# Storing the high and low halves of every stationary matmul operand by turns, element by element

## The chip, the core and the metric

The program runs on one core of one Trainium2 chip. The metric is the device time of one execution in microseconds; the time of the kernel is the median of several executions. A core has TensorE (PE, with its weight loads shown apart as PEld), VectorE (DVE), ScalarE (ACT), GpSimd (POOL) and SyncE (SP), which here only starts transfers. All of them work on SBUF, the on-chip memory of 128 partitions; TensorE writes to PSUM, a smaller memory of 128 partitions.

A matmul on TensorE has two operands in SBUF. The **stationary** one (`lhsT` in the code) is first loaded into the array by a weight load of its own, here 128 columns. The **moving** one (`rhs`) is then streamed past it, one column after the other; its number of columns is the second number of a shape such as 128x256 in the profile.

## The reference

Sliding-window attention with a few sink positions, and behind it a two-layer network with the gate h - tanh(h):

```python
B, H, S, D = 4, 8, 768, 64            # n_sink 4, window 128
scores = q @ k.T / sqrt(D)
keep = is_sink | ((rel >= 0) & (rel < window))
a = softmax(where(keep, scores, -1e9))
x = (a @ v) as [B * S, H * D]         # 3072 tokens x 512
h = x @ w_in                          # 512 -> 2048
g = h - tanh(h)
out = g @ w_out                       # 2048 -> 512
```

## The kernel before

**Splitting numbers.** The inputs are fp32. TensorE has a four-byte type, F32R (`float32r`), that goes through the array in one pass and keeps fewer bits. To keep the accuracy, an operand X is cut into a high part Xh (X cast to F32R) and a low part Xl = X - Xh, and a product is taken as three: Xh Yh + Xl Yh + Xh Yl. ScalarE does the cast (the functions called `high`), VectorE the subtraction (`low`).

**Tiling.** The 3072 tokens are 12 chunks of 256. A chunk's attention is four units, one for each pair of heads. The 2048 inner columns of the network are 8 groups of 256. A *step* is one (chunk, group); there are 96, in the order of lines 262 to 264: the first group for chunks 0, 1 and 2, then chunks 2 and 1 by turns through groups 1 to 7, then chunk 0, then chunks 3 to 11 one after the other.

A step has, on TensorE, 24 matmuls of the first product (`mm1`, line 695: stationary is a 128x128 piece of the first weights, high, high and low; moving is 256 columns of x, high, low and high), written to the PSUM tile h. Then the gate (lines 697 to 717): ACT takes tanh of h (L700), DVE subtracts (L703), ACT casts the result to the high part gh (L707), DVE makes the low part gl (L711). Then come 12 matmuls of the second product (`mm2`, line 743: stationary is a 128x128 piece of gh or gl, moving is 512 columns of the second weights). The first eight of them need only gh, the last four need gl. TensorE does the first product of step n + 1 before the second product of step n.

In the attention, the scores of the units from 12 on are made with F32R as well (line 491: stationary is 128 columns of the split queries qh or ql, moving is 260 columns of the split keys ks). The first twelve units use fp32 as it is (line 484). Lines 570, 601, 618 and 624 are transposes and the product with v.

**Where the halves lie.** The weights come from memory as 64-bit words and are decoded by three DVE instructions (lines 163, 165, 167), which read every second 32-bit word of `wraw`. Then `high` (L671) and `low` (L676) write one tile of [128, 2, 1024]: all the high parts, then all the low parts. gh and gl are two tiles of [128, 2, 256] each. The split queries are one tile of [128, 2, 2, 256], the high half first. In all of these a stationary piece of 128 columns is 128 neighbouring words.

**Order.** A planner (`Work`, lines 176 to 237) gets every piece of work with its engine, a duration and a due time, and lays out a fixed order for each engine. The waits between the engines come from the tiles that the instructions read and write, as the framework sees them.

Of the kernel before, what the change touches and what calls it, by code (L numbers as in the profile page):

```python
# [9 lines left out]
F32 = mybir.dt.float32  # L10
F32R = mybir.dt.float32r
# [3 lines left out]
ALU = mybir.AluOpType  # L15
# [3 lines left out]
P = 128  # L19
DM = H * D  # L20
DFF = 2048
NPAIR = H // 2
# [3 lines left out]
WIN = TS + P  # L26
KW = WIN + TS
KPACK = P + NT * TS
CH = 2 * P
# [5 lines left out]
WG = 2 * DM  # L35
# [134 lines left out]
def _decode(nc, m, t):  # L170
    lo, hi = (w.bitcast(U32) for w in _words(t))
    for i in range(3):
        _decode_part(nc, m.bitcast(U32), lo, hi, i)


class Work:
# [63 lines left out]
def _banded(tc, qd, kp, vp, vs, masks, w_in, w_out, ident, pts, early, out):  # L240
    nc = tc.nc
    et = mybir.EngineType
    with ExitStack() as ctx:
# [195 lines left out]
        def split(u):  # L439

            def k_high(h):
                if h == 0:
                    t = hpool.tile([P, NPAIR * CH], F32R, tag="ha", name=f"ks{u}")
                    ks[u] = t[:, : 2 * KW].rearrange("p (h k) -> p h k", h=2)
                r = slice(64 * h, 64 * h + 64)
                nc.scalar.copy(ks[u][r, h, :], kt[u][r, :])

            def k_low(h):  # L450
                k, t = ks[u], kt[u]
                r, o = slice(64 * h, 64 * h + 64), slice(64 * (1 - h), 64 * (1 - h) + 64)
                nc.vector.tensor_tensor(k[o, h, :], t[r, :], k[r, h, :].bitcast(F32), op=ALU.subtract)  # L453

            def q_high():
                t = hpool.tile([P, 2, 2, CH], F32R, tag="hb", name=f"q{u}")
                qh[u], ql[u] = t[:, 0], t[:, 1]
                nc.scalar.copy(qh[u], qt[u])  # L458

            def q_low():  # L460
                nc.vector.tensor_tensor(ql[u], qt[u], qh[u].bitcast(F32), op=ALU.subtract)

            t = due_unit(u) - 5000
            k, q = ([s] for s in slots(u))
            old = [("x", 2)] + [("xu", 2, i) for i in range(NPAIR)] if u == 3 * NPAIR else []
            work.add("ACT", 525, t, q_high, q, ["qh"] + old)
            work.add("DVE", 705, t, q_low, q + ["qh"], ["ql"], port=True)
            for h in range(2):
                work.add("ACT", 425, t, lambda h=h: k_high(h), k, [("ks", h)] + old)
                work.add("DVE", 590, t, lambda h=h: k_low(h), k, [("ks", h)], port=True)  # L470

        def scores(u, t):
            cc, p, b, c = unit(u)
            kind = min(2 * c + t, 2)
            apart = u < TWO and t == 1

            def products():
                where, tag = (ps_o, "o") if apart else (ps_s, "s")
                both = where.tile([P, 2, 512], F32, tag=tag, name=f"s{u}_{t}")
                ps = [both[:, h, :] for h in range(2)]  # L480
                sps[u, t] = both, ps
                for h in range(2):
                    if raw(u):
                        nc.tensor.matmul(
                            ps[h][:, :WIN], lhsT=qt[u][:, h, t * P : (t + 1) * P],
                            rhs=kt[u][:, t * TS : t * TS + WIN], start=True, stop=True,
                        )
                        continue
                    rhs = ks[u][:, h, t * TS : t * TS + WIN]
                    for i, q in enumerate((qh[u], ql[u])):  # L490
                        nc.tensor.matmul(  # L491
                            ps[h][:, :WIN], lhsT=q[:, h, t * P : (t + 1) * P], rhs=rhs,
                            start=i == 0, stop=i == 1,
                        )

            def merge():
                both, ps = sps[u, t]
                if t == 0:
                    where, tag = (wmpool, "wm") if slot(u) > 1 else (pp, "p")
                    pr[u] = where.tile([P, 4, TS], F32, tag=tag, name=f"p{u}")  # L500
                    st[u] = sm.tile([P, 12], F32, tag="st", name=f"st{u}")
                if kind > 0:
                    nc.vector.copy_predicated(  # L503
                        both[:, :, TS:WIN], above.bitcast(U32).unsqueeze(1).to_broadcast([P, 2, P]),
                        both[:, :, :P],
                    )
                for h in range(2):
                    j = 2 * h + t
                    nc.vector.tensor_tensor_reduce(  # L509
                        out=pr[u][:, j, :], in0=ps[h][:, P:WIN], in1=mask[:, kind, :], scale=-0.125,  # L510
                        scalar=BIG, op0=ALU.add, op1=ALU.min, accum_out=st[u][:, j : j + 1],
                    )

            def exponent():
                for j in (t, 2 + t):
                    e = pr[u][:, j, :]
                    nc.scalar.activation(  # L517
                        e, e, AF.Exp, bias=st[u][:, j : j + 1], scale=-1.0,
                        accum_out=st[u][:, 4 + j : 5 + j],
                    )  # L520

            d = due_unit(u) + 500 * t
            s = ["o0", "o1"] if apart else ["s0", "s1"]
            if raw(u):
                src, took = slots(u), 890
            else:
                src, took = ["qh", "ql", ("ks", 0), ("ks", 1)], 490
            work.add("PE", took, d, products, src, s)
            work.add("DVE", 880 if kind else 450, d + 1000, merge, s + ["mask"] * (0 < kind), [("p", slot(u), i) for i in range(t, 2)])
            work.add("ACT", 780, d + 2000, exponent, (), [("p", slot(u), t)])  # L530
# [128 lines left out]
        def weights(k, g):  # L659
            key, r = (k, g), count[0] % 2  # L660
            count[0] += 1

            wm[key] = pts[:, 2 + r].rearrange("p h a b -> p (h a b)")

            def bits(i):
                lo, hi = (w.bitcast(U32) for w in _words(wraw[key]))
                _decode_part(nc, wm[key].bitcast(U32), lo, hi, i)

            def high():
                t = wpool.tile([P, 2, WG], F32R, tag=f"w{k}_{g}", name=f"w{k}_{g}")  # L670
                nc.scalar.copy(t[:, 0, :], wm[key])  # L671
                wt[key] = t.rearrange("p a (d f) -> p a d f", d=(NPAIR, 2)[k])

            def low():
                t = wt[key].rearrange("p a d f -> p a (d f)")
                nc.vector.tensor_tensor(t[:, 1, :], wm[key], t[:, 0, :].bitcast(F32), op=ALU.subtract)  # L676

            d = due_group(g) + WNEXT * k - WLEAD
            for i in range(3):
                work.add("DVE", (684, 1224, 1224)[i], d, lambda i=i: bits(i), [("wr", k, g, 0), ("wr", k, g, 1)], [("dw", r)], port=True)  # L680
            work.add("ACT", 985, d + 1000, high, [("dw", r)], [("w", *key)])
            work.add("DVE", 1224, d + 1500, low, [("dw", r)], [("w", *key)], port=True)
# [4 lines left out]
        def mm1(n, k):  # L687
            cc, g = order[n]
            if k == 0:
                hps[n] = ps_h.tile([P, 2, CH], F32, tag="h", name=f"h{n}")  # L690
            f, r = divmod(k, 12)
            d, t = divmod(r, 3)
            w = wt[0, g][:, (0, 0, 1)[t], d, f * P : (f + 1) * P]
            x = (xh, xl, xh)[t][cc][:, d, :]
            nc.tensor.matmul(hps[n][:, f, :], lhsT=w, rhs=x, start=r == 0, stop=r == 11)  # L695

        def gate(n):
# [5 lines left out]
                nc.vector.tensor_tensor(hps[n], hps[n], gr[n], op=ALU.subtract)  # L703

            def high():
                gh[n] = gpool.tile([P, 2, CH], F32R, tag="gh", name=f"gh{n}")
                nc.scalar.copy(gh[n], hps[n])  # L707

            def low():
                gl[n] = gpool.tile([P, 2, CH], F32R, tag="gl", name=f"gl{n}")  # L710
                nc.vector.tensor_tensor(gl[n], hps[n], gh[n].bitcast(F32), op=ALU.subtract)  # L711

            d, h, r = due_step(n), ("h", n % 2), n % 2
            work.add("ACT", 510, d, tanh, [h], ["gr"])
# [19 lines left out]
        def mm2(n, k):  # L734
            cc, g = order[n]
            first, last = g == 0, g == NG - 1

            low, r = divmod(k, 8)
            t, r = divmod(r, 2 if low else 4)
            f, i = (r, 2) if low else divmod(r, 2)  # L740
            if first and not low and r == 0:
                ops[cc, t] = sums_of(n, cc, t)
            nc.tensor.matmul(  # L743
                ops[cc, t], lhsT=(gh, gh, gl)[i][n][:, f, t * P : (t + 1) * P],
                rhs=wt[1, g][:, (0, 1, 0)[i], f, :],
                start=first and not low and r == 0, stop=bool(last and low and r == 1),
            )

# [300 lines left out]
```

## Time and profile before

| | us |
|---|---|
| median of 3 executions | 691.68 |
| lowest, highest | 691.46, 692.03 |
| profiled execution, its span | 689.9 |
| PE busy in it | 677.0 |
| PEld busy | 599.9 |
| DVE busy | 427.5 |
| ACT busy | 367.0 |

The profile shows one execution; 1.8 us of the median lie around its span. A matmul's own duration in the profile (0.28 us for 256 columns) is longer than the distance from one matmul to the next, because they are pipelined; what a matmul costs is read from the length of a row of many of them in the chain of work that ended last. PEld is busy beside PE: while one matmul streams, the weights of the next are loaded.

### The profile page before, as it was taken

The page shows a single profiled execution, that of the slowest core. Times are in us where ns is not written, and L with a number is a line of the kernel's source. Part 1 is how long each engine was busy: PE and PEld are TensorE (multiplying, and loading weights), DVE is VectorE, ACT ScalarE, POOL GpSimd, SP SyncE. Part 2 cuts the span into 40 slices and gives each one's busy share as a digit, 9 for nine tenths or more (in the row PEclk, how much of TensorE's full clock was granted, in tenths as well). Part 3 has the DMA queues.
Part 4 walks back from the last instruction along what each step waited for, and adds up shares of the span by engine and source line. Part 5 has one row for each costly group of instructions (what it writes and reads, how often), then busy time and mean ns, then how long its engine had stood idle before and what let it go on. Part 6 is the DMA issues. An engine that isn't in the chain of part 4 may idle for free.

```text
span 689.9 us, 12423 instructions
## 1 busy us (share of the span) xinstructions
PE 677.0 (98%) x4604; PEld 599.9 (87%) x4604; DVE 427.5 (62%) x1084; ACT 367.0 (53%) x1001; POOL 52.0 (8%) x201
## 2 busy tenths in 40 slices
PE   7999999999999999999999999999999999999996
PEld 5777899999889889889988988998898898988985
DVE  7889999847755747556646665565564755663221
ACT  5996433347655646456555655555465545644222
POOL 6220010000000010000001000001000000000000
PEclk9999999999999999999999999999999999999999
DMA  6789800022130121112113112112112212100001
GB/s 205 241 273 384 314 1 5 1 88 55 55 89 28 43 92 55 28 49 84 39 28 109 55 27 90 29 53 85 32 42 75 55 28 61 55 1 1 31 1 35
DMA packets 31713, 52.14 MB, mean 76 GB/s; under 512 B 3228, under 2 KB 21020, under 8 KB 31644
## 3 DMA queue, kind: packets, MB, share of 16 engines
q1 hardware_dynamic: 31340, 50.93, 23.3%
q8 instruction: 38, 0.62, 0.4%
q10 hardware_dynamic: 304, 0.33, 0.2%
q14 instruction: 31, 0.25, 0.1%
HBM read 44.96 MB, written 6.29 MB: 74 GB/s over the span
## 4 chain that ended last, share of the span: by engine, by line
PE 90%; DVE 3%; ACT 3%; SPq 1%; issue 1%; POOL 1%; DMA 0%; POOLq 0%; DVEq 0%; ACTq 0%
PE o L743 39%; PE h L695 38%; PE s L491 5%; PE x L624 5%; PE t L570 2%; ACT p L543 1%; ACT p L517 1%; PE x L618 1%; DVE pt L584 1%; DVE pt L167 1%; DMA qk<-kp 0%; DVE p L509 0%; DVE pt L165 0%; PE x L601 0%; SPq L104 0%
## 5 line engine op out<-in xcount | busy, mean ns | idle before, releaser
L695 PE MATMUL h<-xh,w 128*128 128x256 f32 x1536 | 286.9, 280 | 0.0
L695 PEld LDWEIGHTS h<-xh,w 128*128 128x128 f32 x1536 | 241.1, 188 | 1.9 <-issue 0.2
L695 PE MATMUL h<-xl,w 128*128 128x256 f32 x768 | 214.6, 279 | 0.0
L743 PE MATMUL o<-w,gh 128*128 128x512 f32 x768 | 199.5, 400 | 0.7 <-ACT gh L707 0.6
L743 PEld LDWEIGHTS o<-w,gh 128*128 128x128 f32 x768 | 137.5, 188 | 28.9 <-ACT gh L707 1.5
L695 PEld LDWEIGHTS h<-xl,w 128*128 128x128 f32 x768 | 144.2, 188 | 1.7
L743 PE MATMUL o<-w,gl 128*128 128x512 f32 x384 | 106.8, 398 | 0.0
L700 ACT ACTIVATE graw<-h 128x512 f32<-128x512 f32 x96 | 57.0, 594 | 91.1 <-PE h L695 91.0
L517 ACT ACTIVATE p<-p,st 128x132 f32<-128x132 f32 x192 | 76.1, 398 | 52.6 <-DVE st L509 51.7
L711 DVE TENSOR_TENSOR gl<-h,gh 128x512 fp32r<-128x512 f32 x96 | 66.1, 688 | 48.7 <-ACT gh L707 48.5
L703 DVE TENSOR_TENSOR h<-h,graw 128x512 f32<-128x512 f32 x96 | 66.4, 692 | 44.9 <-ACT graw L700 44.2
L743 PEld LDWEIGHTS o<-w,gl 128*128 128x128 f32 x384 | 70.8, 188 | 16.9 <-issue 1.0
L707 ACT CAST gh<-h 128x512 fp32r<-128x512 f32 x96 | 55.6, 579 | 49.6 <-DVE h L703 49.5
L503 DVE COPY_PREDICATED s<-above,s 128x256 f32<-128x256 uint32 x80 | 34.0, 425 | 75.3 <-PE s L491 74.7
L543 ACT ACTIVATE p<-p,st 128x132 f32<-128x132 f32 x192 | 62.0, 396 | 5.7 <-DVE st L538 5.3
L509 DVE CUSTOM_DVE_ANT_0 p<-s,mask 128x132 f32<-128x132 f32 x192 | 49.0, 292 | 8.2 <-POOL qraw L342 2.1
L548 POOL CAST z<-p 128x16 fp32r<-128x16 f32 x48 | 10.2, 213 | 499.9 <-ACT p L543 498.0
L458 ACT CAST q<-qraw 128x512 fp32r<-128x512 f32 x36 | 22.4, 622 | 45.9 <-PE s L491 43.9
L491 PE MATMUL s<-ks,q 128*128 128x260 f32 x288 | 46.3, 283 | 0.0
L491 PEld LDWEIGHTS s<-ks,q 128*128 128x128 f32 x288 | 42.5, 188 | 4.2
L640 DVE TENSOR_TENSOR xl<-x,xh 128x512 fp32r<-128x512 f32 x24 | 16.5, 689 | 44.9 <-ACT xh L636 44.9
L453 DVE TENSOR_TENSOR ks<-kraw,ks 64x392 fp32r<-64x392 f32 x72 | 40.4, 561 | 2.2
(80 smaller groups left out, 573.8 us busy)
## 6 DMA issues: line engine op xcount, KB each, us to landing
qraw<-qd SPq DMA_DIRECT2D x36, 256.0 KB, 2.7
wraw<-w_in SPq DMA_DIRECT2D x16, 512.0 KB, 8.2
wraw<-w_out SPq DMA_DIRECT2D x16, 512.0 KB, 10.5
kraw<-kp SPq DMA_DIRECT2D x37, 196.0 KB, 2.6
v<-vp SPq DMA_DIRECT2D x27, 256.0 KB, 2.9
out<-ob SPq DMA_DIRECT2D x24, 256.0 KB, 2.2
qk<-kp SPq DMA_DIRECT2D x8, 196.0 KB, 5.1
qk<-qd SPq DMA_DIRECT2D x16, 64.0 KB, 4.9
```

The lines of the kernel that those rows point to most:

```text
L453: nc.vector.tensor_tensor(k[o, h, :], t[r, :], k[r, h, :].bitcast(F32), op=ALU.subtract)
L491: nc.tensor.matmul(ps[h][:, :WIN], lhsT=q[:, h, t * P : (t + 1) * P], rhs=rhs, start=i == 0, stop=i == 1,)
L509: nc.vector.tensor_tensor_reduce(out=pr[u][:, j, :], in0=ps[h][:, P:WIN], in1=mask[:, kind, :], scale=-0.125, scalar=BIG, op0=ALU.add, op1 ...
L517: nc.scalar.activation(e, e, AF.Exp, bias=st[u][:, j : j + 1], scale=-1.0, accum_out=st[u][:, 4 + j : 5 + j],)
L543: nc.scalar.activation(pr[u][:, j, :], pr[u][:, j, :], AF.Copy, scale=s[:, 8 + j : 9 + j])
L624: nc.tensor.matmul(xps[key][(p - p0) // 2][h * 64 : h * 64 + 64, p % 2, a:z], lhsT=vt[cc, i][:, hd : hd + D], rhs=rhs, start=False, stop=p ...
L695: nc.tensor.matmul(hps[n][:, f, :], lhsT=w, rhs=x, start=r == 0, stop=r == 11)
L700: nc.scalar.activation(gr[n], hps[n], AF.Tanh)
L703: nc.vector.tensor_tensor(hps[n], hps[n], gr[n], op=ALU.subtract)
L707: nc.scalar.copy(gh[n], hps[n])
L711: nc.vector.tensor_tensor(gl[n], hps[n], gh[n].bitcast(F32), op=ALU.subtract)
L743: nc.tensor.matmul(ops[cc, t], lhsT=(gh, gh, gl)[i][n][:, f, t * P : (t + 1) * P], rhs=wt[1, g][:, (0, 1, 0)[i], f, :], start=first and no ...
```

## The change

Each stationary operand that comes in two halves is stored so that element i of the high half lies at word 2i and element i of the low half at word 2i + 1 of one tile. This concerns the first weights (`k` = 0), the gate's values (gh and gl become one tile `g`) and the split queries. A stationary piece of 128 columns is now 128 words with a step of two. ACT and DVE write the halves with the same step, and DVE reads the high half with it. The second weights, which are the moving operand, stay as they were, as do x and the keys. The numbers and the order of instructions given to the planner are unchanged.

```diff
--- before.py
+++ after.py
@@ -173,6 +173,12 @@
         _decode_part(nc, m.bitcast(U32), lo, hi, i)
 
 
+def _by_turns(t):
+
+    w = t.rearrange("p (n z) -> p n z", z=2)
+    return w[:, :, 0], w[:, :, 1]
+
+
 class Work:
 
 
@@ -453,12 +459,13 @@
                 nc.vector.tensor_tensor(k[o, h, :], t[r, :], k[r, h, :].bitcast(F32), op=ALU.subtract)
 
             def q_high():
-                t = hpool.tile([P, 2, 2, CH], F32R, tag="hb", name=f"q{u}")
-                qh[u], ql[u] = t[:, 0], t[:, 1]
-                nc.scalar.copy(qh[u], qt[u])
+                t = hpool.tile([P, 4 * CH], F32R, tag="hb", name=f"q{u}")
+                qh[u], ql[u] = _by_turns(t)
+                nc.scalar.copy(qh[u], qt[u].rearrange("p h s -> p (h s)"))
 
             def q_low():
-                nc.vector.tensor_tensor(ql[u], qt[u], qh[u].bitcast(F32), op=ALU.subtract)
+                q = qt[u].rearrange("p h s -> p (h s)")
+                nc.vector.tensor_tensor(ql[u], q, qh[u].bitcast(F32), op=ALU.subtract)
 
             t = due_unit(u) - 5000
             k, q = ([s] for s in slots(u))
@@ -489,7 +496,7 @@
                     rhs = ks[u][:, h, t * TS : t * TS + WIN]
                     for i, q in enumerate((qh[u], ql[u])):
                         nc.tensor.matmul(
-                            ps[h][:, :WIN], lhsT=q[:, h, t * P : (t + 1) * P], rhs=rhs,
+                            ps[h][:, :WIN], lhsT=q[:, (2 * h + t) * P : (2 * h + t + 1) * P], rhs=rhs,
                             start=i == 0, stop=i == 1,
                         )
 
@@ -667,13 +674,13 @@
                 _decode_part(nc, wm[key].bitcast(U32), lo, hi, i)
 
             def high():
-                t = wpool.tile([P, 2, WG], F32R, tag=f"w{k}_{g}", name=f"w{k}_{g}")
-                nc.scalar.copy(t[:, 0, :], wm[key])
-                wt[key] = t.rearrange("p a (d f) -> p a d f", d=(NPAIR, 2)[k])
+                t = wpool.tile([P, 2 * WG], F32R, tag=f"w{k}_{g}", name=f"w{k}_{g}")
+                wt[key] = (t[:, :WG], t[:, WG:]) if k else _by_turns(t)
+                nc.scalar.copy(wt[key][0], wm[key])
 
             def low():
-                t = wt[key].rearrange("p a d f -> p a (d f)")
-                nc.vector.tensor_tensor(t[:, 1, :], wm[key], t[:, 0, :].bitcast(F32), op=ALU.subtract)
+                high, low = wt[key]
+                nc.vector.tensor_tensor(low, wm[key], high.bitcast(F32), op=ALU.subtract)
 
             d = due_group(g) + WNEXT * k - WLEAD
             for i in range(3):
@@ -690,7 +697,7 @@
                 hps[n] = ps_h.tile([P, 2, CH], F32, tag="h", name=f"h{n}")
             f, r = divmod(k, 12)
             d, t = divmod(r, 3)
-            w = wt[0, g][:, (0, 0, 1)[t], d, f * P : (f + 1) * P]
+            w = wt[0, g][(0, 0, 1)[t]][:, (2 * d + f) * P : (2 * d + f + 1) * P]
             x = (xh, xl, xh)[t][cc][:, d, :]
             nc.tensor.matmul(hps[n][:, f, :], lhsT=w, rhs=x, start=r == 0, stop=r == 11)
 
@@ -703,12 +710,13 @@
                 nc.vector.tensor_tensor(hps[n], hps[n], gr[n], op=ALU.subtract)
 
             def high():
-                gh[n] = gpool.tile([P, 2, CH], F32R, tag="gh", name=f"gh{n}")
-                nc.scalar.copy(gh[n], hps[n])
+                t = gpool.tile([P, 4 * CH], F32R, tag="g", name=f"g{n}")
+                gh[n], gl[n] = _by_turns(t)
+                nc.scalar.copy(gh[n], hps[n].rearrange("p f s -> p (f s)"))
 
             def low():
-                gl[n] = gpool.tile([P, 2, CH], F32R, tag="gl", name=f"gl{n}")
-                nc.vector.tensor_tensor(gl[n], hps[n], gh[n].bitcast(F32), op=ALU.subtract)
+                h = hps[n].rearrange("p f s -> p (f s)")
+                nc.vector.tensor_tensor(gl[n], h, gh[n].bitcast(F32), op=ALU.subtract)
 
             d, h, r = due_step(n), ("h", n % 2), n % 2
             work.add("ACT", 510, d, tanh, [h], ["gr"])
@@ -741,8 +749,8 @@
             if first and not low and r == 0:
                 ops[cc, t] = sums_of(n, cc, t)
             nc.tensor.matmul(
-                ops[cc, t], lhsT=(gh, gh, gl)[i][n][:, f, t * P : (t + 1) * P],
-                rhs=wt[1, g][:, (0, 1, 0)[i], f, :],
+                ops[cc, t], lhsT=(gh, gh, gl)[i][n][:, (2 * f + t) * P : (2 * f + t + 1) * P],
+                rhs=wt[1, g][(0, 1, 0)[i]][:, f * DM : (f + 1) * DM],
                 start=first and not low and r == 0, stop=bool(last and low and r == 1),
             )
```

## The prediction

> **What bounds the kernel now.** I read the page's busy table first, then its shares of the chain that ended last, then the table of stretches.
>
> ```profile
> span 689.9 us, 12423 instructions
> PE 677.0 (98%) x4604; PEld 599.9 (87%) x4604; DVE 427.5 (62%) x1084; ACT 367.0 (53%) x1001; POOL 52.0 (8%) x201
> PE o L743 39%; PE h L695 38%; PE s L491 5%; PE x L624 5%; PE t L570 2%; ACT p L543 1%; ACT p L517 1%; PE x L618 1%; DVE pt L584 1%; DVE pt L167 1%; DMA qk<-kp 0%; DVE p L509 0%; DVE pt L165 0%; PE x L601 0%; SPq L104 0%
> ...
> core 0: us, PE busy (x) PEld busy (x) DVE busy (x) ACT busy (x) POOL busy (x), PEclk, DMA share, GB/s
> 60.00:138.00 78.00, 77.39 (x508) 69.12 (x507) 73.99 (x86) 30.41 (x46) 2.77 (x3) 1.00 0.31 119
> 138.00:640.00 502.00, 501.95 (x3505) 450.11 (x3504) 292.60 (x778) 275.30 (x753) 27.32 (x117) 1.00 0.18 53
> ```
>
> TensorE is busy for 501.95 of the 502 us between 138 and 640, at the full granted clock, and two lines carry 77% of the chain: both have a stationary operand that the change touches. L491 is the third such line, with 5%. So what counts is the distance from one matmul to the next, and it is read from rows of the chain in order of time, where nothing else stands between:
>
> ```profile
> 79.44 2.73 PE h L695 x24
> 82.17 2.79 PE o L743 x12
> 84.96 2.83 PE h L695 x24
> ...
> 244.60 2.05 PE h L695 x18
> ...
> 256.80 3.53 PE h L695 x30
> ...
> 679.01 5.62 PE o L743 x24
> ...
> L695 PE MATMUL h<-xh,w 128*128 128x256 f32 x1536 | 286.9, 280 | 0.0
> L695 PE MATMUL h<-xl,w 128*128 128x256 f32 x768 | 214.6, 279 | 0.0
> L743 PE MATMUL o<-w,gh 128*128 128x512 f32 x768 | 199.5, 400 | 0.7 <-ACT gh L707 0.6
> L743 PE MATMUL o<-w,gl 128*128 128x512 f32 x384 | 106.8, 398 | 0.0
> L491 PE MATMUL s<-ks,q 128*128 128x260 f32 x288 | 46.3, 283 | 0.0
> ```
>
> A matmul of 256 columns takes 2.83 / 24 = 0.118 us (3.53 / 30 is the same), one of 512 columns 5.62 / 24 = 0.234 us: twice as much for twice the columns. So the distance follows the moving stream, not the weight load, which has 128 columns in both. But there is a second pace: 2.73 / 24 = 0.114 us at 79.44, where chunk 2 is at work (its x lies in another pool than that of the other chunks, line 632), and 2.05 / 18 = 0.114 us in a stretch of chunk 3 with the usual x. The pace of L695 thus has two settings, 3.5% apart. By the counts in the page's groups, the whole of L695 is (1536 + 768) x 0.118 = 272 us, of L743 (768 + 384) x 0.234 = 270 us.
>
> Where does the weight load stand in this? It can be seen alone where TensorE had run dry:
>
> ```profile
> 70.74 0.30 PEld L743 LDWEIGHTS o<-w,gh 128*128 128x128 f32 x2 [0.51 <-ACT gh L707]
> L743 PEld LDWEIGHTS o<-w,gh 128*128 128x128 f32 x768 | 137.5, 188 | 28.9 <-ACT gh L707 1.5
> ```
>
> Two loads end 0.30 us after the first began and one is recorded with 0.188, so the second began 0.30 - 0.188 = 0.11 us after the first: that is what a load occupies. Under a 512-column matmul it is hidden with 0.12 us to spare. Under a 256-column matmul 0.118 - 0.11 = 0.008 us is left, and less, about 0.004, at the faster pace.
>
> Is the stream slowed by the load that runs beside it? The end of the program has one matmul under which nothing is loaded:
>
> ```profile
> 683.05 1.09 PE L743 MATMUL o<-w,gh 128*128 128x512 f32 x4
> 683.25 0.58 ACT L754 COPY ob<-o 128x512 f32<-128x512 f32 x1 [2.19 <-PE o L743]
> 683.98 0.63 PE L743 MATMUL o<-w,gl 128*128 128x512 f32 x2
> 684.65 0.58 ACT L754 COPY ob<-o 128x512 f32<-128x512 f32 x1 [0.82 <-PE o L743]
> ```
>
> The copy at 683.25 waits for the matmul one before 683.05, begun at 683.05 - 0.234 = 682.82, with a load beside it: 0.43 us from start to copy. The copy at 684.65 waits for the last matmul, begun at 683.98 + 0.234 = 684.21, with no load beside it: 0.44 us. A 512-column stream is not quicker alone. For 256 columns no such pair is as clear, and the two paces leave the question open there.
>
> **The change, part by part.** *L743, 1152 loads with a step of two words.* The stream sets 0.234 us whether a load runs or not, and a load may double (0.22) before it shows. Cost 0; were that cover gone, every 0.01 us per load would be 11.5 us.
>
> *L695 and L491, 2304 + 288 loads.* No stationary operand in this trace is read with a step, so the load's new duration is bounded: below, it cannot gain by itself, since the stream of 0.114 to 0.118 us covers it; above, it costs as if it passed over 256 words, 2 x 0.11 = 0.22 us, and then sets the pace: 2592 x (0.22 - 0.118) = 264 us. I take 0, because the nearest row, a DVE read of every second word, shows no loss:
>
> ```profile
> L165 DVE SCALAR_TENSOR_TENSOR pt<-wraw,pt 128x1024 uint32<-128x1024 uint32 x16 | 19.7, 1228 | 0.1
> L676 DVE TENSOR_TENSOR w<-pt,w 128x1024 fp32r<-128x1024 f32 x16 | 19.5, 1222 | 0.7 <-ACT w L671 0.7
> L711 DVE TENSOR_TENSOR gl<-h,gh 128x512 fp32r<-128x512 f32 x96 | 66.1, 688 | 48.7 <-ACT gh L707 48.5
> ```
>
> L165 reads `wraw` with a step of two words, L676 reads neighbours; both have two inputs and 1024 elements, and they take 1228 and 1222 ns.
>
> *The pace of L695.* If new addresses move all chunks to the 0.114 setting, 2304 - 192 = 2112 matmuls (without chunk 2) gain 2.83 - 2.73 = 0.10 us per 24: 8.8 us. If the pace fell to the load's 0.11, it would be 2112 x 0.008 + 192 x 0.004 = 17.7 us. The other way, chunk 2 falling back, costs 8 x 0.10 = 0.8 us. I take 0, since the moving operands keep their addresses and the one thing that visibly goes with the pace is the pool of x.
>
> *Writes with a step.* ACT casts (L671, L707, L458) and DVE subtractions (L676, L711, L461) now write every second word. No row shows such a write. Lower bound 0; upper bound twice the elements: a 512-word subtraction would take L676's 1.22 in place of 0.69 us, L676 itself 1.22 + 1024/512 x (1.22 - 0.69) = 2.28 us. After 138 us DVE is 58% busy (292.60 of 502) and hides it. Between 60 and 138 us it is not hidden; this is one round of two steps' work there:
>
> ```profile
> 105.21 0.70 DVE L703 TENSOR_TENSOR h<-h,graw 128x512 f32<-128x512 f32 x1
> 105.81 0.68 DVE L163 TENSOR_SCALAR pt<-wraw 128x1024 uint32<-128x1024 uint32 x1
> 106.41 1.22 DVE L676 TENSOR_TENSOR w<-pt,w 128x1024 fp32r<-128x1024 f32 x1
> 107.55 0.69 DVE L711 TENSOR_TENSOR gl<-h,gh 128x512 fp32r<-128x512 f32 x1
> 110.82 0.70 DVE L703 TENSOR_TENSOR h<-h,graw 128x512 f32<-128x512 f32 x1 [0.20 <-ACT graw L700]
> ...
> 130.46 1.23 DVE L676 TENSOR_TENSOR w<-pt,w 128x1024 fp32r<-128x1024 f32 x1
> 135.21 0.80 PE h L695 x7
> ```
>
> Of 5.6 us DVE idles 0.20. The last first-layer weights are ready at 131.7 and used at about 135.2, so 3.5 us of lead are left at the end. At the upper bound gl adds 0.53 us per round and L676 1.06 in every second round (only half the weights are first-layer): 1.06 on average, less 0.20 idle, over some 11 rounds is 9.5 us, less the lead 6 us. I take 0, by the read of L165.
>
> [...]
>
> *The tile g.* gh and gl were two tiles and are now one, with elements by turns. The second product's first eight matmuls need gh alone and often start before gl is done. If the framework compares only the range from first to last word, these matmuls wait for gl:
>
> ```profile
> 56.00 1.20 PE L743 MATMUL o<-w,gh 128*128 128x512 f32 x4
> 56.29 0.68 DVE L711 TENSOR_TENSOR gl<-h,gh 128x512 fp32r<-128x512 f32 x1
> ...
> 285.46 0.69 DVE L711 TENSOR_TENSOR gl<-h,gh 128x512 fp32r<-128x512 f32 x1 [0.94 <-ACT gh L707]
> 286.11 2.11 PE L743 MATMUL o<-w,gh 128*128 128x512 f32 x8
> ...
> DVE pt L584 <- ACT pt L577: 4.4, 9, 0.7
> ```
>
> At 56.00 gl ends 0.97 us after gh's matmuls began, at 286.11 only 0.04 us after. Taken through all 96 steps, gl ends later than that start in 48, by 16.7 us together. Bounds: 0 and 16.7 us; I take 0, since the views are disjoint word by word.
>
> **Sum.** 689.9 + 0 for each part = 689.9 us of span, with the 1.8 us around it **691.7 us**.
>
> **The rivals.** *The pace falls (faster).* Loads with a new step meet the stream differently, and L695 runs at 0.114 everywhere: 691.7 - 8.8 = **682.9**, at the load's floor 674.0. For it speaks that the setting changes inside chunk 3 with no address changed, so something besides x sets it; against it, that 512 columns show no effect of a load at all. Chance 0.30, of which 0.07 for something below 674 that these rows do not explain.
>
> *A wait between the halves (slower).* The price is 16.7 us, **708.4**; it decides as soon as gl's end lies behind the start of gh's matmuls, as at 56.00. For it: L584 waits for L577 in nine cases although they write different blocks, lying by turns, of one tile pt. Against it: both also read the same PSUM tile, which may be the reason. Chance 0.13.
>
> *Stepped writes fill DVE (slower).* **697.7** at the bound; it decides once a round grows by more than its 0.20 us idle and 3.5 / 11 = 0.32 us of lead. Chance 0.07.
>
> *The load grows (slower).* It decides from 0.008 us per load on; at the bound 691.7 + 264 = **956**, and each 0.004 us beyond costs 10 us. Chance 0.10, most of it far outside.
>
> **How the numbers follow.** No change 0.40, forecast 691.7. A measurement here can tell about 0.2%, 1.4 us, from nothing. Faster 0.30, slower 0.13 + 0.07 + 0.10 = 0.30. The range reaches down to the load's floor (674) and up over the full wait (709); outside remain the 0.07 below, most of the load's 0.10 and some of the pieces: about 0.2. Faster and same together hold most of the chance; the forecast's own range is 690.3 to 693.1.
>
> **What would show it.** Right: rows of L695 with x24 at 2.83 us, of L743 with x24 at 5.62, a lone load still 0.11 us, L711 and L676 at 688 and 1222 ns, PE busy all through 138 to 640. The faster case shows as 2.73 or less in the rows of chunks 3 to 11. The wait shows as a new row "PE o L743 <- DVE" in the list of waits. Stepped writes show in the means of L711 and L707. A longer load shows in the distance of L695 while L743 stays. If L743 itself falls below 0.234, my reading that the load does not touch a 512-column stream is wrong.

## The result, and the profile after

The changed kernel takes 697.54 us (median of 4 runs, 697.16 to 698.30) against 691.86 us (4 runs, 691.46 to 692.04): a ratio of 1.0084, with a 95% interval of 1.0070 to 1.0099. It is slower by 0.8%. The forecast was no change, 691.7. The whole range, 674 to 709, held the time; the forecast's own band, 690.3 to 693.1, did not.

The first fence has rows of the changed kernel's page: span, busy times, then groups (busy us, mean ns of one | idle time before them).

```profile
span 695.6 us, 12410 instructions
PE 682.7 (98%) x4604; PEld 616.2 (89%) x4604; DVE 428.6 (62%) x1084; ACT 372.6 (54%) x1001; POOL 52.2 (8%) x201
...
L702 PE MATMUL h<-xh,w 128*128 128x256 f32 x1536 | 294.7, 284 | 0.0
L751 PE MATMUL o<-w,g 128*128 128x512 f32 x1152 | 289.5, 398 | 0.5 <-ACT g L715 0.5
L702 PEld LDWEIGHTS h<-xh,w 128*128 128x128 f32 x1536 | 251.3, 197 | 1.5 <-issue 0.2
L751 PEld LDWEIGHTS o<-w,g 128*128 128x128 f32 x1152 | 216.4, 195 | 36.7 <-issue 1.5
...
L719 DVE TENSOR_TENSOR g<-h,g 128x512 fp32r<-128x512 f32 x96 | 66.2, 690 | 50.6 <-ACT g L715 50.3
...
L715 ACT CAST g<-h 128x512 fp32r<-128x512 f32 x96 | 59.2, 616 | 49.0 <-DVE h L710 48.7
```

The lines have moved by seven or eight: the first product is L702 (L695 before), the second L751 (L743), the scores L498 (L491), the gate's cast L715 (L707) and its subtraction L719 (L711). The span grew by 5.7 us and PE's busy time by the same 5.7, so nothing waits longer; the matmuls themselves take longer. The loads of both lines are recorded 7 to 9 ns longer (188 before). DVE's subtraction kept its time (690 for 688), ACT's cast takes 616 for 579 ns. This is the cast's row on the page of the kernel before:

```profile
L707 ACT CAST gh<-h 128x512 fp32r<-128x512 f32 x96 | 55.6, 579 | 49.6 <-DVE h L703 49.5
```

The weights' cast pays too; here it is in the groups by line of the kernel before, then of the changed one:

```profile
L671 ACT CAST w<-pt 128x1024 fp32r<-128x1024 f32 x16 | 16.8, 1051 | 4.1 <-DVE pt L167 4.1
```

```profile
L679 ACT CAST w<-pt 128x1024 fp32r<-128x1024 f32 x16 | 17.5, 1095 | 3.9 <-DVE pt L167 3.8
```

The 44 ns between these two means are spread over 16 casts, of which only the eight of the first weights write with a step. By their own durations in the two traces, those eight went from 1054 to 1142 ns, 87 more, and the other eight stayed at 1048.

The chain of waits of the changed kernel, in order of time (start us, us, what), has the distances:

```profile
79.75 2.88 PE h L702 x24
82.63 2.78 PE o L751 x12
85.41 2.91 PE h L702 x24
...
259.19 3.64 PE h L702 x30
...
684.78 5.54 PE o L751 x24
```

The first product goes at 2.88 to 2.91 us per 24, 0.120 to 0.121 us each; the two settings of before (2.83 and 2.73) have gone. What is left is a smaller pair: about half of the 96 steps have a mean distance near 0.120 us, as at 79.75, and half between 0.121 and 0.122, as at 85.41. The second product went the other way: 5.54 for 5.62, 0.231 us.

To price this, I took the starts of neighbouring matmuls of the same line from the two traces and added up their distances: 260.4 to 267.7 us for the first product (2209 distances), 248.2 to 246.3 for the second (1042), 25.7 to 26.1 for the scores (216). That is +7.3 - 1.9 + 0.4 = +5.8 us, the whole difference of the spans. What has to be explained is a loss of 7.3 and a gain of 1.9, not one loss of 5.7.

A lone load is seen again where TensorE had run dry, in PEld's timeline of the changed kernel:

```profile
71.02 0.31 PEld L751 LDWEIGHTS o<-w,g 128*128 128x128 f32 x2 [0.37 <-ACT g L715]
```

Two loads end after 0.31 us, and the second is recorded with 0.197: it began 0.115 us after the first, by the starts in the trace. The same place of the kernel before gives 0.108.

And the wait between the halves? Timelines of PE and of DVE in the changed kernel, where the prediction had looked:

```profile
56.14 1.66 PE L751 MATMUL o<-w,g 128*128 128x512 f32 x6
```

```profile
56.43 0.68 DVE L719 TENSOR_TENSOR g<-h,g 128x512 fp32r<-128x512 f32 x1
```

The low half is being written to the tile until 57.11, while matmuls that read its high half have run since 56.14. The same holds in 48 of the 96 steps, as before. There is no such wait.

### The profile page after: what moved, and what is told of

It is laid out like the page before. It is cut to its first block, busy times and chain, and to the rows that moved or that the text cites. A ratio compares the mean times of both kernels' runs of the same rounds, so it can differ in the third digit from the quotient of the medians.

```text
span 695.6 us, 12410 instructions
## 1 busy us (share of the span) xinstructions
PE 682.7 (98%) x4604; PEld 616.2 (89%) x4604; DVE 428.6 (62%) x1084; ACT 372.6 (54%) x1001; POOL 52.2 (8%) x201
## 4 chain that ended last, share of the span: by engine, by line
PE 90%; ACT 4%; DVE 2%; SPq 1%; issue 1%; POOL 1%; DMA 0%; POOLq 0%; ACTq 0%
PE h L702 38%; PE o L751 38%; PE s L498 5%; PE x L631 5%; PE t L577 2%; ACT p L550 1%; ACT p L524 1%; PE x L625 1%; DMA qk<-kp 0%; DVE pt L165 0%; PE x L608 0%; SPq L104 0%; ACT zr L615 0%; POOL vraw L427 0%; PE s L491 0%
## 5 line engine op out<-in xcount | busy, mean ns | idle before, releaser
L702 PE MATMUL h<-xh,w 128*128 128x256 f32 x1536 | 294.7, 284 | 0.0
L751 PE MATMUL o<-w,g 128*128 128x512 f32 x1152 | 289.5, 398 | 0.5 <-ACT g L715 0.5
L702 PEld LDWEIGHTS h<-xh,w 128*128 128x128 f32 x1536 | 251.3, 197 | 1.5 <-issue 0.2
L751 PEld LDWEIGHTS o<-w,g 128*128 128x128 f32 x1152 | 216.4, 195 | 36.7 <-issue 1.5
L702 PE MATMUL h<-xl,w 128*128 128x256 f32 x768 | 217.9, 284 | 0.0
L702 PEld LDWEIGHTS h<-xl,w 128*128 128x128 f32 x768 | 151.1, 197 | 1.4
L707 ACT ACTIVATE graw<-h 128x512 f32<-128x512 f32 x96 | 57.0, 594 | 93.8 <-PE h L702 93.2
L719 DVE TENSOR_TENSOR g<-h,g 128x512 fp32r<-128x512 f32 x96 | 66.2, 690 | 50.6 <-ACT g L715 50.3
L715 ACT CAST g<-h 128x512 fp32r<-128x512 f32 x96 | 59.2, 616 | 49.0 <-DVE h L710 48.7
L498 PEld LDWEIGHTS s<-ks,q 128*128 128x128 f32 x288 | 43.8, 196 | 3.5
L498 PE MATMUL s<-ks,q 128*128 128x260 f32 x288 | 46.6, 285 | 0.0
L631 PE MATMUL x<-pt,v 128*64 128x128 f32 (+1 forms) x512 | 41.5, 316 | 0.0
L631 PEld LDWEIGHTS x<-pt,v 128*64 128x64 f32 x512 | 31.0, 137 | 11.8 <-issue 4.9
```

Of the source, the lines that this page charges most:

```text
L498: nc.tensor.matmul(ps[h][:, :WIN], lhsT=q[:, (2 * h + t) * P : (2 * h + t + 1) * P], rhs=rhs, start=i == 0, stop=i == 1,)
L631: nc.tensor.matmul(xps[key][(p - p0) // 2][h * 64 : h * 64 + 64, p % 2, a:z], lhsT=vt[cc, i][:, hd : hd + D], rhs=rhs, start=False, stop=p ...
L707: nc.scalar.activation(gr[n], hps[n], AF.Tanh)
L715: nc.scalar.copy(gh[n], hps[n].rearrange("p f s -> p (f s)"))
L719: nc.vector.tensor_tensor(gl[n], h, gh[n].bitcast(F32), op=ALU.subtract)
L751: nc.tensor.matmul(ops[cc, t], lhsT=(gh, gh, gl)[i][n][:, (2 * f + t) * P : (2 * f + t + 1) * P], rhs=wt[1, g][(0, 1, 0)[i]][:, f * DM : ( ...
```

## The experiments

Each is the kernel before with one edit. All distances in this table are means between the starts of neighbouring matmuls of a line in the run's own trace (waits of more than 15% over the median left out), in ns; "lone load" is the distance between two loads where TensorE had run dry, of the operand in question. A ratio is to runs of the kernel before on the same chip beside it (medians 691.83 to 692.18).

| kernel | us | ratio, 95% interval | first product | second | scores | lone load |
|---|---|---|---|---|---|---|
| before | 691.86 | | 117.5 | 233.3 | 118.8 | 108 |
| all by turns (the change) | 697.54 | 1.0084, 1.0070 to 1.0099 | 120.7 | 231.0 | 120.6 | 115 |
| w_turns | 698.77 | 1.0103, 1.0088 to 1.0119 | 120.7 | 233.3 | 119.1 | |
| g_turns | 688.44 | 0.9952, 0.9939 to 0.9966 | 116.9 | 231.0 | 119.0 | 115 |
| q_turns | 693.03 | 1.0011, 1.0002 to 1.0020 | 117.4 | 233.3 | 121.0 | |
| g_halves | 692.16 | 1.0002, 0.9993 to 1.0011 | 117.5 | 233.2 | 118.7 | 109 |
| w_step4 | 951.01 (one run) | | 231.5 | 233.2 | 119.6 | 212 |
| g_step4 | 718.77 (one run) | | 117.4 | 237.6 | 119.6 | 212 |
| g_step3 | 700.90 (one run) | | 117.5 | 233.5 | 119.2 | 164 |
| x_shift | 687.26 | 0.9930, 0.9916 to 0.9943 | 115.1 | 233.0 | 119.6 | 108 |
| x_shift_w | 697.27 (one run) | | 120.1 | 233.2 | 119.4 | |
| x_shift_g | 686.09 | 0.9914, 0.9901 to 0.9928 | 115.3 | 230.9 | 119.1 | 115 |
| g_mixed | 692.04 (one run) | | 117.8 | 232.8 | 118.3 | 115 |

### One part at a time

**w_turns** has the first weights alone by turns, **g_turns** the gate's values alone, **q_turns** the queries alone. The edits are the hunks of the change's diff that name `wt`, `gh` and `gl`, or `qh` and `ql`; the core of each is the same line:

```diff
-                wt[key] = t.rearrange("p a (d f) -> p a d f", d=(NPAIR, 2)[k])
...
+                wt[key] = (t[:, :WG], t[:, WG:]) if k else _by_turns(t)
```

> Only the first weights by turns; gate values and queries as before. Theory A (a load with a step of two words occupies TensorE's load path 0.116 us in place of 0.108, and with 256 moving columns that load now sets the distance): the first product goes to 0.1205 us per matmul, the second stays at 0.2335, and the time is 691.9 + 2304 x 0.003 = 698 to 699 us, longer than with the whole change. Theory B (no longer load, only other addresses that meet the stream differently): the exposed load stays at 0.108 and the first product may lie anywhere from 0.114 to 0.122. Theory C (the longer casts of ACT are the loss): eight casts of the weights grow by 0.1 us each and are hidden, so 692 us.

> Only the gate's values by turns; weights and queries as before. Theory A: the first product keeps 0.1178 us per matmul, the second goes to the 0.2305 of the changed kernel because its longer load is hidden there, and the time falls by about 1152 x 0.0028 = 3 us less some 1 us of waits for the longer cast: 689 to 690.5 us. Theory C: the cast of 0.616 in place of 0.579 us stands on the way to the second product in about half of the steps: 692 to 695.5 us. Theory B: both paces may change, since where gh and gl lie has changed.

> Only the split queries lie by turns. Theory (a step-2 load costs 0.007 us more and the scores are bound by their loads): the scores' pace goes from 0.1188 to 0.1205 us, 288 matmuls give +0.3 to +0.5 us, 692.2 us, the cast of the high part 0.622 to 0.667 us, and both products keep 0.1175 and 0.2333 us. With w_turns (+6.9) and g_turns (-3.4, of which 1.3 are steps of the first product that changed their pace and that load-bound steps do not have) the three parts then add up to the change's +5.7. Rival (the parts act on one another): q_turns alone gives more than 1 us either way.

Chains of w_turns, then of g_turns:

```profile
79.82 2.87 PE h L701 x24
...
85.49 2.88 PE h L701 x24
...
685.92 5.62 PE o L749 x24
```

```profile
73.83 2.72 PE h L701 x24
79.31 2.83 PE h L701 x24
...
675.81 5.53 PE o L750 x24
```

Each product changes its pace with its own operand. With the weights by turns the first product goes at 2.88 per 24 and the second keeps 5.62; with the gate by turns the second goes at 5.53 and the first keeps its two settings, though chunks 1 and 2 have traded them (before, 79.44 had 2.73). By steps: mean distance under 115.5 ns in 10 of 96 steps before, in 18 here. Against the before of the same runs (691.83 and 692.18), the parts come to +6.9 us (w_turns), -3.4 (g_turns) and +0.9 (q_turns, 0.1 to 1.4 by its interval; the forecast of 0.3 to 0.5 lies inside, the scores' 0.1210 a little above the 0.1205 expected). Together +4.4, where the change gives +5.7. The 1.3 us between are first-product time: it fell from 260.4 to 259.1 us in g_turns, by the steps that changed their setting, while with the weights by turns it is 267.7 us whether the gate's values lie by turns (the change) or not (w_turns). The time of w_turns is as theory A had it; that of g_turns lies 0.6 us below its 689 to 690.5, which had the first product unchanged. So the change is a loss of 7 us in one operand and a gain of 2 us in another, thrown together.

**g_halves** keeps g_turns' single tile but not the step:

```diff
-                gh[n], gl[n] = _by_turns(t)
+                gh[n], gl[n] = t[:, : 2 * CH], t[:, 2 * CH :]
```

> The gate's values in one tile as in the change, but high half first and low half behind it, so that a stationary piece is 128 neighbouring words again. Theory S (the step of two in the loads is what quickens the second product): its distance goes back to 0.2333 us, ACT's cast to 0.579 us, and the time to that of the kernel before, 691.9 us. Rival P (it was the place of the halves, one tile of 4 KiB instead of two of 2 KiB): the distance stays at 0.231 and the time at 688 to 689 us, or lower as the cast is short again.

It is the kernel before again (ratio 1.0002), in both products. What acts in g_turns is the step, not the merged tile.

### What a load pays for its step

If the load is what holds the first product, a longer load must hold it longer. **w_step4** puts the weights' elements four words apart (the two halves of two column blocks by turns), **g_step4** the gate's. **g_step3** puts three of the gate's four pieces three words apart.

```diff
+                    v = t.rearrange("p (d c f z) -> p d f c z", d=NPAIR, f=2, z=2)
+                    wt[key] = v[:, :, :, :, 0], v[:, :, :, :, 1]
...
+                v = t.rearrange("p (f c t z) -> p f t c z", f=2, t=2, z=2)
+                gh[n], gl[n] = v[:, :, :, :, 0], v[:, :, :, :, 1]
...
+    three = t[:, z * 3 * P : (z + 1) * 3 * P].rearrange("p (c j) -> p j c", j=3)
```

> [...] Theory B: no more than with a step of two, 690 to 700 us.

> The gate's values with a step of four words; the rest as before. Theory A: the load grows further but is hidden behind 0.23 us of stream as long as it stays under that, so the second product is at 0.2305 or a little less, and the time is that of the gate by turns alone, plus what the longer writes of ACT and DVE cost. If a load of 0.2 us and more shows, the second product rises above 0.234.

> Three of the four 128-column pieces of gh and of gl lie by turns with a step of 3 words, the fourth is contiguous; ACT and DVE write each round's gate in two instructions. [...] Rival (any step beyond 8 bytes costs what step 4 does): 0.212 us. By both the load stays under the 0.231 to 0.237 us of a 512-column matmul, so the time is set by the pace of the second product and by the doubled number of casts and subtractions: 688 to 700 us by the theory, 700 to 725 by the rival.

Rows of w_step4: PEld's timeline, the chain in order of time, and a group of its page.

```profile
32.81 0.55 PEld L706 LDWEIGHTS h<-xh,w 128*128 128x128 f32 x2 [0.77 <-DVE w L687]
```

```profile
236.46 5.59 PE h L706 x24
...
342.70 6.99 PE h L706 x30
```

```profile
L706 PEld LDWEIGHTS h<-xh,w 128*128 128x128 f32 x1536 | 439.9, 328 | 2.7 <-DVE w L687 0.8
```

Two loads now begin 0.212 us apart and a 256-column matmul takes 5.59 / 24 = 0.233 us at 236.46, as long as one of 512 columns. The stream did not change, so it is the load that sets the distance, though the distance stays 0.02 us above the lone load (0.2315 in the mean, against 0.212). The program takes 951 us, where the expectation had 690 to 700 by its theory B.

PEld's timelines of g_step4, then of g_step3, each with two lone loads:

```profile
72.48 0.54 PEld L751 LDWEIGHTS o<-w,g 128*128 128x128 f32 x2 [0.81 <-ACT g L715]
```

```profile
71.48 0.42 PEld L758 LDWEIGHTS o<-w,g 128*128 128x128 f32 x2 [0.59 <-ACT g L720]
```

The second load begins 0.212 us after the first with a step of four words, 0.164 with three, 0.115 with two and 0.108 with one. A load of 128 neighbouring words pays 0.108 / 128 = 0.84 ns a word. With a step of four it passes over 512 words and pays 0.212 / 512 = 0.414 ns for each, about half as much. With a step of three it passes over 384: 384 x 0.414 = 0.159, measured 0.164. With a step of two it passes over 256: 0.106, measured 0.115. So by an estimate from these four loads, a load takes 0.84 ns for each word that it brings or 0.414 for each that it passes over, whichever is more, to within 3 to 8%. At a step of two the two are level (0.108 and 0.106), and it still takes 0.007 us more than neighbouring words. Those 0.007 us are what this case is about.

Under 512 columns the same lengths hardly show. At 0.164 the second product is back at 233.5 ns; at 0.212 it takes 237.6, with 0.02 us of cover left. That pace explains 1152 x 0.0043 = 5 of g_step4's 27 us. Most of the rest seems to go to writers that have become slow, and through which the chain now passes; this is read from the chain and was not tested apart. The page of g_step4 has the chain by line, and the two writers among its groups:

```profile
PE o L751 37%; PE h L701 31%; PE x L630 5%; PE s L497 4%; ACT g L715 3%; ACT p L549 2%; ACT p L523 2%; PE t L576 2%; DVE g L719 1%; DVE pt L590 1%; DVE h L709 1%; PE x L624 1%; DVE p L515 1%; DMA qk<-kp 0%; ACT graw L706 0%
...
L719 DVE TENSOR_TENSOR g<-h,g 128x512 fp32r<-128x512 f32 x96 | 105.4, 1098 | 79.1 <-ACT g L715 78.2
...
L715 ACT CAST g<-h 128x512 fp32r<-128x512 f32 x96 | 104.2, 1086 | 64.4 <-DVE h L709 64.4
```

A write with a step of four words costs DVE 1098 for 688 ns and ACT 1086 for 579. In g_step3 both write twice per step; its 700.9 us lie at the border between the two ranges of its forecast. Both ranges rest on a load that stays under the stream, and it did: 0.164 us, not the rival's 0.212, under 0.2335.

### The two settings of the first product

**x_shift** leaves every stationary operand where it is and moves x 4480 bytes down, by making its pool earlier (the two small pools `pp` and `sm`, now behind it, move up); **x_shift_g** and **x_shift_w** do this to g_turns and w_turns.

```diff
+        xpool = pool("xpool", 2)
         pp, sm = pool("pp", 2), pool("sm", 4)
-        xpool, gpool = pool("xpool", 2), pool("gpool", 2)
+        gpool = pool("gpool", 2)
```

> The kernel before, with one edit: the pool of x is laid out ahead of two small pools, so that x lies 4480 bytes lower, with the same remainder by 4096 as the x of chunk 2; all stationary operands stay where they are. Theory D (the two settings of the first product, 0.1178 and 0.1138 us, come from how the addresses of moving and stationary operand stand to each other): all chunks run at 0.1138 and the time falls by 8.8 us to 683. Rival E (chunk 2 is quick for another reason, such as its neighbours or its data): the first product stays at 0.1178 outside chunk 2 and the time at 691.9.

> Both edits that may help: the gate's values by turns with a step of two, and x 4480 bytes lower. If the two act on different matmuls, the gains add: 691.9 - 3.4 - 8.8 = 679.7 us under theory D, 688.4 under rival E.

> The first weights by turns, and x 4480 bytes lower. Theory A (with a step of two the first product goes at the pace of its loads): where x lies does not matter any more, the distance is 0.1205 as without the shift and the time 698 to 699 us. If the stream still set the pace, the shift would lower it by 0.004 us per matmul, to 690.

Chains of x_shift, of x_shift_g and of x_shift_w in the same stretch:

```profile
79.42 2.83 PE h L696 x24
...
85.05 2.74 PE h L696 x24
```

```profile
79.45 2.75 PE h L702 x24
...
84.97 2.75 PE h L702 x24
```

```profile
79.77 2.88 PE h L702 x24
...
85.44 2.88 PE h L702 x24
```

Moving x makes the kernel before 0.7% faster (692.02 to 687.26 beside it, ratio 0.9930): 66 of the 96 steps now go at the quick setting, against 10, and the first product falls from 260.4 to 255.2 us. But chunk 2, whose x did not move, has become slow (79.42), and chunk 1 quick (85.05). So where x and the small pools lie matters, but no simple distance between x and the weights of a step fixes its setting; the time lies between theory D (683) and rival E (691.9), and neither holds. Nor do the addresses of a step's own operands fix it alone: g_turns and g_mixed (below) leave x and the first weights where they were, and have 18 quick steps and none. With the weights by turns the same move gives 1.5 us where it gave 4.8: 697.27 us against the 698.77 of w_turns, with all 96 steps between 119.6 and 120.4 ns, so the upper one of the small pair of settings has gone. The two gains add up only in part. x_shift_g has the second product at 246.3 us, as in g_turns, but the first at 255.7, no lower than in x_shift. It takes 686.09 us, 5.9 under the kernel before, where 4.8 + 3.4 would be 8.2. This is 0.9%, the fastest version here.

### What quickens the second product

**g_mixed** has the pieces of t = 0 by turns and those of t = 1 contiguous, within the same steps.

```diff
+    turns = t[:, : 2 * CH].rearrange("p (n z) -> p n z", z=2)[:, :, z]
+    return turns.rearrange("p (f c) -> p f c", f=2), t[:, (2 + z) * CH : (3 + z) * CH].rearrange("p (f c) -> p f c", f=2)
```

> Which matmul does a step-2 load quicken: the one that streams beside it, or the one whose weights it brings? Of the gate's four 128-column pieces the two of t = 0 lie by turns, the two of t = 1 are contiguous; ACT and DVE write in two instructions each. In the 12 matmuls of a step the weights of numbers 0 to 3 and 8, 9 then have step 2, those of 4 to 7 and 10, 11 step 1. The distance from matmul i to i + 1 is the time of stream i, with load i + 1 beside it. Theory (the load beside the stream): the distances 0, 1, 2, 7 and 8 are near 0.231, those of 3 to 6, 9 and 10 near 0.2333. Rival (the weights' own layout): 0 to 3, 8 and 9 near 0.231, 4 to 7 and 10 near 0.2333; the two differ at 3, 7 and 9. A third outcome: all are alike, and then neither the load nor the weights set it matmul by matmul.

In the 63 steps whose twelve matmuls stand in one row, the eleven mean distances are 232.6, 232.1, 232.1, 231.3, 232.8, 232.6, 234.0, 232.5, 232.7, 234.4 and 234.4 ns. Of the three that tell the theories apart (the count starts at 0), number 3 is quick as the weights' own layout wants, number 7 is between, and number 9 is slow as the load beside it wants. Neither holds; single distances run from 225 to 236. This was inconclusive.

## Why the prediction was right and wrong

**What bounds the kernel: right.** The distances between matmuls made up the whole difference, 5.8 us by their sum where the span grew by 5.7. That the forecast of no change came within 0.8% is luck in part: two terms that it had at 0 came out at +7.3 and -1.9 us.

**L695 and L491, taken as 0: this step failed, by its size.** The prediction named the mechanism (the load grows), the place (under 256 columns) and a threshold (0.008 us per load). But it took the load's growth as 0, from the row of a DVE read with a step of two words, which showed no loss. The lone load grew by 0.007 us, and the first product went from 0.1175 to 0.1207: (267.7 - 260.4) us over 2209 distances is 0.0033 us each, or 7.6 us for all 2304. Two numbers were too kind. The row of DVE did not carry over to TensorE's reads: a step of two words cost DVE 6 of 1222 ns, 0.5%, and the load 0.007 of 0.108 us, 6%. And the cover was counted from a lone load: 0.007 us is less than the threshold of 0.008, and yet it showed. In a row of matmuls the distance is longer than the lone load of the same kind: 0.1207 against 0.115, and 0.2315 against 0.212 in w_step4. A load 0.007 us longer moved the distance by 0.0033, so by an estimate (that what goes beyond the margin is paid in full) the margin was not 0.008 but 0.007 - 0.0033, about 0.004 us. L491 missed in the same way and by less: its distance went from 0.1188 to 0.1206, 0.4 us in all.

**The load at its bound: right in kind, and the near number is luck.** The 956 are for loads of 256 words in L695 and L491 together; w_step4 steps the weights of L695 alone, for which the same sum gives 691.7 + 2304 x (0.22 - 0.118) = 927. It measured 951, since the distance did not go to the load's 0.212 but to 0.2315.

**L743, cost 0: wrong in sign.** It fell from 0.2333 to 0.2310, a gain of 1.9 us in the change and in g_turns. The prediction said what this would mean: its reading that a load does not touch a 512-column stream is wrong. The reading came from one pair at the end of the program (0.43 and 0.44 us), with 0.01 us of resolution against an effect of 0.002.

**The pace of L695 has two settings: right, and it could have been worth something.** The rival at 682.9 did not come about, because a row with step-two loads goes at 0.1195 to 0.1217 us by steps, above both settings. The setting does move, however, when x moves (x_shift, 66 quick steps against 10) and when the gate's layout alone does (g_turns, 18). The prediction's floor, the load's 0.11, was reached nowhere: the quickest steps in any run are at 0.1133.

**Stepped writes, 0: right for DVE** (688 to 690 ns for the gate; for the weights 1222 to 1223, a mean over stepped and unstepped writes). ACT pays 37 ns on the gate, 6%, and 87 on the first weights (1054 to 1142), 8%. TensorE waited no longer for the gate's cast than before (0.5 us in all, 0.6 before). With a step of four words, in g_step4, the subtraction took 1.098 us, where a step of two left it at 0.690. So here the price begins between the two.

**A wait between the halves, 0: right.** The matmuls of the high half run while the low half is written to the same tile, and g_halves, which has that single tile too, takes the time of before.

**What stays open.** Why a step-two load quickens a 512-column stream by 1% (233.3 to 231.0 ns), while a step of three does not (233.5), and what picks the setting of the first product. Both answer to where data lies, which suggests that load and stream meet in the memory; that is argued from these runs, not shown, and g_turns and g_mixed speak against a setting that a step's own operands fix. It is open too whether the quick setting of before, 0.1133, is the pace of the stream or already that of loads of 0.108: a row of step-two loads, too, goes about 0.005 us above the lone load.

## What to carry to other kernels

Where a weight load hides under a short stream, compare the two to the nanosecond before you touch the stationary operand's layout: 0.007 us more per load made the first product 3% slower, since the cover was about 4 ns by the estimate above, while a second product with 0.12 us of cover took the same layout at a gain of 1.9 us. Split a change that touches several operands and time each alone: this one was +6.9, -3.4 and +0.9. And read a duration from the resource in question: the same step of two words cost DVE's read 0.5% and the weight load 6%.

## What was not expected of the hardware

The distance of equal matmuls at full clock (0.997 to 1.000 in these runs) depends on where the data lies. Moving x by 4480 bytes and two small pools with it, with no instruction changed, was worth 4.8 us. Matmuls of 256 columns with contiguous weights went at 0.1133 or at 0.1178 us, some steps at a mean between, and steps switched from one to the other. And a load two words apart, though 0.007 us longer, made the 512-column stream beside it shorter, 0.2333 to 0.2310.
